# Loading the K and V cache of a decode step in two halves from two queues

## The chip, the cores and the metric

The kernel runs on one core of a Trainium2 chip. The core has five engines that run side by side: TensorE (PE in the profile, with its weight loads as PEld), VectorE (DVE), ScalarE (ACT), GpSimd (POOL) and SyncE (SP). Sixteen DMA engines move data between the device memory (HBM) and the on-chip memory. A DMA is issued by an instruction of SP, ACT or POOL and goes into that engine's DMA queue; the profile calls SP's queue q1 and ACT's q10. The metric is the device time of one execution in microseconds.

## The reference

One token goes through a layer of a transformer. With h the input row of 512 numbers and a cache of 65536 earlier positions:

```
xn = layernorm(x)                                   x: 1 x 512
q  = xn @ wq                                        32 query heads of 128, in 8 groups of 4
p  = softmax(q @ k_cache.T * 128**-0.5)             per group of 4: k_cache 65536 x 128
o  = p @ v_cache                                    v_cache 65536 x 128
h  = x + o @ wo
out = h + ((hn @ w_gate) * (hn @ w_up)) @ w_down    hn = layernorm(h), w_gate and w_up 512 x 1792
```

All of it is float32. The two caches hold 8 x 65536 x 128 numbers each, 268 MB each; they are read once and nothing of them is used twice.

## The kernel before

**Tiling.** The host puts the caches into one array of 64 chunks. For each of the 8 groups (`HKV`, called heads below) there are four K chunks and four V chunks (`NT`), each of 128 partitions times 16384 numbers: 64 KB in each partition, 8.39 MB in all. They are called K0 to K3 and V0 to V3 below. On the chip there are two buffers of that size, `kv[0]` and `kv[1]`. The even chunks go to `kv[0]`, the odd ones to `kv[1]`.

**TensorE.** Each chunk is used by 32 windows, written by `windows` (line 364): a window is 512 columns of the chunk, shows as two matmul records (64 per chunk), and window 0 comes first. A K chunk gives scores, collected in a bank of PSUM (`ps`). After the four K chunks come the softmax steps, and the weights that result (`st`, line 261) multiply the V chunks. `windows` can wait for a semaphore ahead of its first window; a chunk of K is written as windows 0 to 16, 16 to 24, 24 to 28 and 28 to 32, a chunk of V as 0 to 8, 8 to 12, 12 to 16, 16 to 24, 24 to 28 and 28 to 32. The waits between these parts are used for the last chunk and for the feed-forward weights, which come in several loads. For the other chunks one load brings the whole chunk and raises `s_k0` or `s_v0`, and POOL has raised the other semaphores (`s_k16`, `s_v16` and so on) at the start, by as much as all these chunks will take from them (line 133).

**Handing back a buffer.** When the last window of a chunk is through (`kd`), VectorE raises `free` (lines 237, 270, 279). SyncE waits for `free` and then issues the load of the chunk after next into that buffer. So there are always at most two chunks on their way or in use.

**SyncE.** SyncE's program is lines 121 and 141 to 174: the first query weights, chunks 0 and 1, then one load per `free`. Once per head it also waits for `wf` and loads `wqo_sb`, 16 KB in each partition (2.10 MB): the next head's part of `wq` and this head's part of `wo` (line 148). By its place in the loop this load goes into the queue behind the load of V1 and ahead of the load of V2. The last chunk comes in four loads (line 160), then the gate and up weights (`gu`) and the down weights (`wd`), into the same two buffers.

**ScalarE.** Per head ScalarE copies the four score banks to `sc` (line 216), each when VectorE has raised `pa` right behind `free`. Then it computes two exponentials (line 220) when VectorE has raised `da` for the first time, and two more when it has raised it for the second time, which is when V1 is through. It issues one small DMA at the start, for `x_row` (line 109).

Of the kernel before, what the change touches and what calls it, by code (L numbers as in the profile page):

```python
# [10 lines left out]
HKV, REP, DH = 8, 4, 128  # L11
SK = 65536
CK = 16384
NT = SK // CK
# [6 lines left out]
LAST = HKV - 1  # L21
PE_ONLY, DVE_ONLY, ACT_ONLY, SP_ONLY = (bass.OrderedEngineSet([e]) for e in (
    mybir.EngineType.PE, mybir.EngineType.DVE, mybir.EngineType.Activation, mybir.EngineType.SP))
SIDE = 9
LATE = 1
DVE_ACT = bass.OrderedEngineSet([mybir.EngineType.DVE, mybir.EngineType.Activation])
K_CUTS = (0, 4, 8, 12, 16, 32)
V_CUTS = (0, 8, 12, 16, 24, 28, 32)
# [14 lines left out]
def body(nc, xr, kvd, wq0, wqo, wo7, gu, wd, out):  # L43
    pe_e, dve_e, act_e, pool_e, sp = nc.tensor, nc.vector, nc.scalar, nc.gpsimd, nc.sync
# [17 lines left out]
    kv = [tile(f"kv{i}", P, CK, align=1024) for i in range(2)]  # L62
# [23 lines left out]
    def sem(name):  # L86
        sems.append(nc.alloc_semaphore(name))
        return sems[-1]
# [6 lines left out]
    pa, da, free, wf = (sem(n) for n in ("pa", "da", "free", "wf"))  # L95
    s_k0, s_k16, s_k24, s_k28 = (sem(f"s_k{i}") for i in (0, 16, 24, 28))
    s_v0, s_v8, s_v16, s_v24, s_v28 = (sem(f"s_v{i}") for i in (0, 8, 16, 24, 28))
    s_wq, s_w = sem("s_wq"), sem("s_w")
    s_wd = [sem(f"s_wd{i}") for i in range(NC - SIDE)]
    s_xr = sem("s_xr")  # L100
    late, s_act, s_pool, s_y, s_a, s_out = (sem(n) for n in ("late", "s_act", "s_pool", "s_y", "s_a", "s_out"))
    gu_t = kv[0].rearrange("p (k x) -> p k x", k=KT)[:, :, 0:2 * F]
    wd_t = kv[1]
    end = 2 * HKV * NT

    def take(e, s, n=1):
        e.wait_ge(s, n).then_inc(s, -n)  # L107
# [4 lines left out]
        inst.then_inc(own, 1)  # L112
        take(dve_e, own)

    def even(g):
        sp.dma_start(kv[0], kvd[g]).then_inc(s_k0, 16)

    def odd(g):
        sp.dma_start(kv[1], kvd[g]).then_inc(s_v0, 16)

    sp.dma_start(wq_sb, wq0).then_inc(s_wq, 16)
    pe_e.br("pe_main")
# [7 lines left out]
        out=ident, in_=ident, compare_op=ALU.not_equal, fill=1.0, base=0,  # L130
        pattern=[[-1, P]], channel_multiplier=1))
    pool.tick(pool_e.memset(qx, 0.0))
    for p, w, n in ((s_k16, 16, 0), (s_k24, 16, 0), (s_k28, 16, 0), (s_v8, 17, 0),
                    (s_v16, 16, -1), (s_v24, 16, -1), (s_v28, 16, -1)):
        pool_e.sem_inc(p, w * (end // 2 + n))
    for t in (o_pad, f_pad, sel_pad, acc, y):
        c_pads = pool.tick(pool_e.memset(t, 0.0))
    pool_e.wait_ge(s_act, 1).then_inc(s_pool, 1)
    pool_e.br("fin")

    even(0)
    odd(1)
    for g in range(2, 6):
        take(sp, free)
        (odd if g % 2 else even)(g)
    with nc.Fori(0, LAST, engines=SP_ONLY) as h:
        take(sp, wf)
        sp.dma_start(wqo_sb, wqo[h]).then_inc(s_w, 16)
        with nc.Fori(0, 2 * NT, 2, engines=SP_ONLY) as c:
            for i, put in enumerate((even, odd)):  # L150
                take(sp, free)
                put(c + (h * (2 * NT) + 6 + i))
    take(sp, wf)
    sp.dma_start(wo_sb, wo7).then_inc(s_w, 16)
    take(sp, free)
    even(end - 2)
    take(sp, free)
    for lo, hi, p in ((0, 16, s_v0), (16, 24, s_v16), (24, 28, s_v24), (28, 32, s_v28)):
        cs = slice(lo * 512, hi * 512)
# [50 lines left out]

    o_blocks = bass.AP(tensor=ptp[1].tensor, offset=0, ap=[list(ptp[1].ap[0]), [1, REP], [132, 4], [32, 4]])
    qd = qx.rearrange("p (j x) -> p j x", j=4)
    with nc.Fori(0, HKV, engines=DVE_ACT):
        for s in range(NT):
            take(act_e, pa)
            act_e.copy(sc[s], ps[s % 2]).then_inc(ad, 1)  # L216
        for n in range(0, NT, 2):
            take(act_e, da)
            for s in range(n, n + 2):
                act_e.activation(  # L220
                    ex[s - n], sc[s], AF.Exp, bias=nbias[:, 0:1], scale=SCALE,
                    accum_out=sums[:, s:s + 1]).then_inc(atok[s - n], 1)
        take(dve_e, pd)
        dve_e.tensor_copy(qrow, ptp[0][0:1, :]).then_inc(tok, 1)  # L224
        take(dve_e, pd)
        dve_e.sem_inc(wf, 1)
        q4 = sm[0][:, 0:REP]
        dve_e.tensor_copy(
            qd[:, :, 0:252].rearrange("p j (r x) -> p j r x", x=36)[:, :, :, 0:REP],
            q4.unsqueeze(1).unsqueeze(1).to_broadcast([P, 4, 7, REP])).then_inc(own, 1)  # L230
        dve_e.tensor_copy(
            qd[:, :, 252:256], q4.unsqueeze(1).to_broadcast([P, 4, REP])).then_inc(own, 1)
        take(dve_e, own, 2)
        dve_e.tensor_copy(st, qx.rearrange("p (g c) -> p g c", c=32)).then_inc(qt, 2)
        for s in range(NT):
            take(dve_e, kd, 1 + s % 2)
            dve_e.sem_inc(free, 1)
            dve_e.sem_inc(pa, 1)
            take(dve_e, ad)
            if s < 2:  # L240
                dve_e.sem_inc(qt, 1)
            dve_e.tensor_reduce(out=mx[:, s:s + 1], in_=sc[s], axis=AX.X, op=ALU.max).then_inc(own, 1)  # L242
        take(dve_e, own, NT)
        dve_e.tensor_reduce(out=m1, in_=mx, axis=AX.X, op=ALU.max).then_inc(tok, 1)  # L244
        dve_e.memset(st[:, :, 16:32], 0.0).then_inc(own, 1)
        take(dve_e, pd)
        dve_e.tensor_reduce(
            out=mrow, in_=sm[1][0:1, 0:P].rearrange("p (g h) -> p h g", h=REP), axis=AX.X,
            op=ALU.max).then_inc(own, 1)
        take(dve_e, own, 2)  # L250
        dve_e.tensor_copy(mexp, mrow.unsqueeze(1).to_broadcast([1, 32, REP])).then_inc(tok, 1)  # L251
        take(dve_e, pd)
        dve_e.tensor_scalar(
            out=nbias, in0=sm[0][:, 0:1], scalar1=-SCALE, scalar2=None, op0=ALU.mult).then_inc(da, 1)
        for n in range(NT):
            if n == 2:
                dve_e.sem_inc(tok, 2)
                take(dve_e, pd, 2)
                dve_e.sem_inc(da, 1)
            take(dve_e, pd)  # L260
            dve_e.tensor_copy(  # L261
                st[:, :, 0:16].rearrange("p g (b h) -> p b g h", h=REP),
                ptp[n % 2].rearrange("p (b g h) -> p b g h", b=4, h=REP)).then_inc(qt, 1)
            if n == NT - 1:
                mine(dve_e.tensor_reduce(out=l1, in_=sums, axis=AX.X, op=ALU.add))
                dve_e.tensor_scalar(
                    out=l4, in0=sel_h, scalar1=l1[:, 0:1], scalar2=None, op0=ALU.mult).then_inc(tok, 1)
            take(dve_e, kd, 1 + n % 2)
            if n < NT - 1:
                dve_e.sem_inc(free, 1)  # L270
            if n == 0:
                mine(dve_e.tensor_copy(orow, ps[0]))  # L272
            elif n < NT - 1:
                mine(dve_e.tensor_tensor(out=orow, in0=ps[n % 2], in1=orow, op=ALU.add))  # L274
            else:
                for cs in (slice(0, 256), slice(256, 512)):
                    dve_e.tensor_tensor(  # L277
                        out=orow[:, cs], in0=ps[1][:, cs], in1=orow[:, cs], op=ALU.add).then_inc(tob, 1)
        dve_e.sem_inc(free, 1)
        take(dve_e, pd)  # L280
        mine(dve_e.reciprocal(linv, sm[1][:, 0:REP]))
        take(dve_e, pd)
        mine(dve_e.tensor_reduce(out=ored, in_=o_blocks, axis=AX.XY, op=ALU.add))
        dve_e.tensor_tensor(out=o_pad[:, :, 0], in0=ored, in1=linv, op=ALU.mult).then_inc(tok, 1)  # L284
        take(dve_e, pd)
        for half, p in ((0, tok), (1, s_a)):
            cs = slice(half * 256, half * 256 + 256)
            dve_e.scalar_tensor_tensor(  # L288
                out=acc[:, cs], in0=attn[:, cs], scalar=1.0, in1=acc[:, cs], op0=ALU.mult, op1=ALU.add,
                accum_out=rsum[:, half:half + 1]).then_inc(p, 1)  # L290
# [40 lines left out]
    for o, g, u in ((f_pad[:, 0:1, 0], gux[0][:, 0, 3:4, 0], uf[:, 0, 1, 3:4, 0]),  # L331
                    (f_pad[:, 1:4, 0], gux[1][:, 1, 0:3, 0], uf[:, 1, 1, 0:3, 1]),
                    (f_pad[:, 4:5, 0], gux[1][:, 0, 3:4, 0], uf[:, 1, 1, 3:4, 0])):
        i = dve_e.scalar_tensor_tensor(
            out=o, in0=g, scalar=ln_r3[:, 0:1], in1=u, op0=ALU.mult, op1=ALU.mult)
# [7 lines left out]
    dve.n += 1  # L343
    assert dve.n == LATE
    dve_e.sem_inc(dve.sem, 1)
# [7 lines left out]
    for k in range(KT):  # L353
        if k == KT - 1:
            pe_e.wait_ge(s_wq, 16)
        i = pe_e.transpose(ps[0][:, k:k + 1], xn_row[0:1, k * P:(k + 1) * P], ident[0:1, 0:1])
# [35 lines left out]
    for k in range(KT):  # L392
        i = mm(ptp[0][0:1, :], xn[:, k:k + 1], wq_sb[:, k, :], start=(k == 0), stop=(k == KT - 1))  # L393
    i.then_inc(pd, 1)
    pe_e.wait_ge(tok, 4)
    for r in range(REP):
        i = pe_e.transpose(sm[0][:, r:r + 1], qrow[0:1, r * P:(r + 1) * P], ident[0:1, 0:1])  # L397
# [13 lines left out]
    for half in range(2):  # L411
        pe_e.wait_ge(atok[half], 1)
        for b in range(4):
            i = pe_e.transpose(ptp[half][:, b * P:(b + 1) * P], ex[half][:, b * P:(b + 1) * P], ident)  # L414
# [9 lines left out]
    for half in range(2):  # L424
        step()
        for b in range(2):
            i = pe_e.transpose(ptp[half][:, b * P:(b + 1) * P],
                               gu_sb[:, (2 * half + b) * P:(2 * half + b + 1) * P], ident)
# [25 lines left out]
    for b in range(4):  # L454
        if b < 3:
            pe_e.wait_ge(*((tob, 1), (s_w, 16), (tob, 2))[b])
        i = pe_e.transpose(ptp[1][:, b * P:(b + 1) * P], orow[:, b * P:(b + 1) * P], ident)  # L457
    i.then_inc(pd, 1)
    pe_e.wait_ge(tok, 2)
    for r in range(REP):  # L460
        i = mm(attn[32 * r:32 * r + 32, :], o_pad[:, r, :], wo_sb[:, r, :],  # L461
               start=True, stop=True)
# [6 lines left out]
    for k in range(KT):  # L469
        if k % 2 == 0:  # L470
            pe_e.wait_ge(*((s_a, HKV) if k else (tok, 3)))
        i = pe_e.transpose(ptp[1][:, k * P:(k + 1) * P], acc[:, k * P:(k + 1) * P], ident)
# [69 lines left out]
```

## Time and profile before

| | |
|---|---|
| time, median of 3 runs | 1308.68 us (1308.65 to 1309.05) |
| span of the profiled execution, first to last instruction | 1307.4 us |
| between that span and the median of the runs | 1.3 us |
| bytes read from HBM | 564.66 MB |
| packets on SP's queue q1 / on ACT's queue q10 | 12848 / 2 |
| busy PE, DVE, ACT, POOL | 686.2, 111.6, 54.9, 2.7 us |
| PE waiting for a K or V load (line 364) | 520.1 us, 58 times |

The page gives the span of the profiled execution and no separate time for it; the runs' times lie 1.3 us above that span. A DMA issue has a row of its own (SPq or ACTq); its time is that of the issuing instruction, not of the transfer. When a chunk has landed is seen from the row of line 364 that had waited for it. "Packets" are the pieces that the DMA engines recorded.

### The profile page before, as it was taken

How to read it: one execution, taken by the hardware profiler on the slowest of the kernel's cores; microseconds unless marked ns; L12 is line 12 of the kernel's file. 1: busy time of each engine (PE TensorE's matmuls, PEld its weight loads, DVE VectorE, ACT ScalarE, POOL GpSimd, SP SyncE). 2: the span in 40 equal slices, each digit the busy share in tenths (PEclk: the TensorE clock that was granted, in tenths of full speed). 3: DMA queues.
4: the chain of work that ended last, by engine and by line, in shares of the span. 5: the costliest groups of instructions: out<-in, count | busy, mean ns of one | idle time of the engine just before them, and what ended most of it. 6: DMA issues, size and time to landing. Idle time of an engine off the chain costs nothing. (4 is left out here: it accounts for less than half of the span.)

```text
span 1307.4 us, 10833 instructions
## 1 busy us (share of the span) xinstructions
PE 686.2 (52%) x4610; PEld 191.5 (15%) x4610; DVE 111.6 (9%) x286; ACT 54.9 (4%) x106; POOL 2.7 (0%) x12
## 2 busy tenths in 40 slices
PE   4456364453654545553554636535566445545557
PEld 1011111110111111111110211101111111111112
DVE  1000010100101001000010101001010010100101
ACT  0000000000000000000000000000000000000000
POOL 0000000000000000000000000000000000000000
PEclk8676796776976768767787767868677677877679
DMA  9999999999999999999999999999999999999999
GB/s 417 421 445 429 437 447 419 449 417 449 417 449 417 449 417 449 421 445 427 439 439 427 449 417 449 417 449 417 449 417 449 417 434 440 441 437 429 447 408 382
DMA packets 12850, 564.72 MB, mean 432 GB/s; under 512 B 1409, under 2 KB 1457, under 8 KB 2610
## 3 DMA queue, kind: packets, MB, share of 16 engines
q1 hardware_dynamic: 12848, 564.71, 99.8%
q10 hardware_dynamic: 2, 0.00, 0.0%
HBM read 564.66 MB, written 0.05 MB: 432 GB/s over the span
## 5 line engine op out<-in xcount | busy, mean ns | idle before, releaser
L364 PE MATMUL ps<-kv,st 128*32 128x512 f32 x4184 | 591.0, 728 | 534.6 <-DMA kv<-in_kv 520.1
L364 PEld LDWEIGHTS ps<-kv,st 128*32 128x32 f32 x4184 | 146.7, 131 | 962.3 <-DMA kv<-in_kv 568.1
L242 DVE TENSOR_REDUCE mx<-sc 128x1 f32<-128x512 f32 x32 | 21.9, 686 | 535.9 <-DVEq L107 535.9
L414 PE MATMUL ptp<-ident,ex 128*128 128x128 f32 x128 | 27.3, 372 | 19.8 <-ACT ex L220 19.5
L216 ACT COPY sc<-ps 128x512 f32<-128x512 f32 x32 | 18.8, 586 | 444.6 <-ACTq L107 444.5
L274 DVE TENSOR_TENSOR orow<-ps,orow 128x512 f32<-128x512 f32 x16 | 11.1, 691 | 298.3 <-DVEq L107 298.3
L220 ACT ACTIVATE ex<-sc,nbias 128x512 f32<-128x512 f32 x32 | 22.8, 714 | 304.4 <-ACTq L107 304.4
L393 PE MATMUL ptp<-wqo_sb,xn 128*1 128x512 f32 x64 | 30.4, 620 | 6.4 <-DVE acc L288 5.0
L216 ACT ACT_TABLE_LOAD x8 | 10.3, 1283 | 441.5 <-ACTq L107 441.5
L261 DVE COPY st<-ptp 128x512 f32<-128x512 f32 x32 | 22.1, 692 | 44.5 <-DVEq L107 44.5
L414 PEld LDWEIGHTS ptp<-ident,ex 128*128 128x128 f32 x128 | 20.2, 188 | 22.9 <-ACT ex L220 22.8
L407 PE MATMUL sm<-ident,m 128*1 128x128 f32 x16 | 4.5, 283 | 27.2 <-DVE m L244 17.6
L277 DVE TENSOR_TENSOR orow<-ps,orow 128x256 f32<-128x256 f32 x16 | 6.0, 419 | 129.3 <-DVEq L107 129.3
L272 DVE COPY orow<-ps 128x512 f32<-128x512 f32 x8 | 5.5, 692 | 102.0 <-DVEq L107 102.0
L461 PE MATMUL attn<-wqo_sb,o_pad 128*32 128x512 f32 x64 | 8.5, 605 | 5.9 <-DVE o_pad L284 5.9
L409 PE MATMUL sm<-ones,mexp 1*128 1x1 f32 x32 | 6.9, 281 | 6.7 <-DVE mexp L251 6.7
L393 PEld LDWEIGHTS ptp<-wqo_sb,xn 128*1 128x1 f32 x64 | 4.9, 85 | 30.9 <-issue 18.1
L224 DVE COPY qrow<-ptp 1x512 f32<-1x512 f32 x8 | 5.4, 679 | 29.7 <-DVEq L107 29.7
L457 PE MATMUL ptp<-ident,orow 128*128 128x128 f32 x32 | 6.1, 300 | 3.0 <-DVE orow L277 3.0
L407 PEld LDWEIGHTS sm<-ident,m 128*1 128x1 f32 x16 | 1.3, 79 | 41.8 <-DVE m L244 24.9
L288 DVE SCALAR_TENSOR_TENSOR acc<-attn,acc 128x256 f32<-128x256 f32 x16 | 6.2, 421 | 10.8 <-DVEq L107 10.8
L397 PE MATMUL sm<-ident,qrow 1*128 1x1 f32 x32 | 3.2, 201 | 7.1 <-DVE qrow L224 7.1
(84 smaller groups left out, 78.4 us busy)
## 6 DMA issues: line engine op xcount, KB each, us to landing
wqo_sb<-in_wqo SPq DMA_DIRECT2D x7, 2048.0 KB, 32.9
kv<-in_kv SPq DMA_DIRECT2D x1, 4096.0 KB, 22.2
kv<-in_gu SPq DMA_DIRECT2D x1, 3584.0 KB, 17.6
kv<-in_kv SPq DMA_DIRECT2D x1, 2048.0 KB, 26.7
kv<-in_kv SPq DMA_DIRECT2D x2, 1024.0 KB, 29.7
kv<-in_gu SPq DMA_DIRECT2D x1, 1792.0 KB, 21.4
kv<-in_wd SPq DMA_DIRECT2D x1, 1536.0 KB, 19.0
kv<-in_wd SPq DMA_DIRECT2D x5, 256.0 KB, 20.5
```

The costliest lines, as they stand in the source:

```text
L216: act_e.copy(sc[s], ps[s % 2]).then_inc(ad, 1)
L220: act_e.activation(ex[s - n], sc[s], AF.Exp, bias=nbias[:, 0:1], scale=SCALE, accum_out=sums[:, s:s + 1]).then_inc(atok[s - n], 1)
L242: dve_e.tensor_reduce(out=mx[:, s:s + 1], in_=sc[s], axis=AX.X, op=ALU.max).then_inc(own, 1)
L261: dve_e.tensor_copy(st[:, :, 0:16].rearrange("p g (b h) -> p b g h", h=REP), ptp[n % 2].rearrange("p (b g h) -> p b g h", b=4, h=REP)).the ...
L274: mine(dve_e.tensor_tensor(out=orow, in0=ps[n % 2], in1=orow, op=ALU.add))
L288: dve_e.scalar_tensor_tensor(out=acc[:, cs], in0=attn[:, cs], scalar=1.0, in1=acc[:, cs], op0=ALU.mult, op1=ALU.add, accum_out=rsum[:, hal ...
L364: i = mm(ps[buf][32 * j:32 * j + 32, :], st[:, 8 * j + r, :], kv[buf][:, w * 512:(w + 1) * 512], start=(r == 0), stop=(r in (2, 3, 7)), sk ...
L393: i = mm(ptp[0][0:1, :], xn[:, k:k + 1], wq_sb[:, k, :], start=(k == 0), stop=(k == KT - 1))
L409: mm(sm[0][:, 0:1], mexp.rearrange("p g h -> p (g h)"), ones[0:1, 0:1], start=True, stop=True).then_inc(pd, 1)
L414: i = pe_e.transpose(ptp[half][:, b * P:(b + 1) * P], ex[half][:, b * P:(b + 1) * P], ident)
L457: i = pe_e.transpose(ptp[1][:, b * P:(b + 1) * P], orow[:, b * P:(b + 1) * P], ident)
L461: i = mm(attn[32 * r:32 * r + 32, :], o_pad[:, r, :], wo_sb[:, r, :], start=True, stop=True)
```

## The change

The loads of chunks 2 to 61 are each cut into two loads of 32 KB per partition, columns 0 to 8191 and 8192 to 16383. SyncE still waits for `free`; it then raises a new semaphore `af` and issues the first half, which raises `s_k0` or `s_v0`. ScalarE waits for `af` and issues the second half, which raises `s_k16` or `s_v16`, so that windows 16 and on now wait for a load of their own. Chunks 0, 1 and 62 are cut in the same way, but both loads come from SyncE. Chunk 63 and the feed-forward weights stay as they were.

ScalarE's loop over the heads becomes a function: behind each copy of scores it issues the second half of the chunk that is loaded in that place, and behind each pair of exponentials those of two chunks more. The last head is written out behind the loop because its V chunks free buffers for loads that SyncE issues alone. VectorE's loop is a loop of its own now, with the same instructions. POOL no longer raises `s_k16` and `s_v16` at the start.

```diff
-    def even(g):
-        sp.dma_start(kv[0], kvd[g]).then_inc(s_k0, 16)
-
-    def odd(g):
-        sp.dma_start(kv[1], kvd[g]).then_inc(s_v0, 16)
+    def both(g):
+        for lo, p in ((0, (s_k0, s_v0)[g % 2]), (HALF, (s_k16, s_v16)[g % 2])):
+            sp.dma_start(kv[g % 2][:, lo:lo + HALF], kvd[g][:, lo:lo + HALF]).then_inc(p, 16)
...
-    for p, w, n in ((s_k16, 16, 0), (s_k24, 16, 0), (s_k28, 16, 0), (s_v8, 17, 0),
-                    (s_v16, 16, -1), (s_v24, 16, -1), (s_v28, 16, -1)):
+    for p, w, n in ((s_k24, 16, 0), (s_k28, 16, 0), (s_v8, 17, 0),
+                    (s_v24, 16, -1), (s_v28, 16, -1)):
...
-    even(0)
-    odd(1)
+    both(0)
+    both(1)
+
+    def first_half(g, i):
+        take(sp, free)
+        sp.sem_inc(af, 1)
+        sp.dma_start(kv[i][:, 0:HALF], kvd[g][:, 0:HALF]).then_inc((s_k0, s_v0)[i], 16)
+
+    def second_half(g, i):
+        take(act_e, af)
+        act_e.dma_start(kv[i][:, HALF:CK], kvd[g][:, HALF:CK]).then_inc((s_k16, s_v16)[i], 16)
+
     for g in range(2, 6):
-        take(sp, free)
-        (odd if g % 2 else even)(g)
+        first_half(g, g % 2)
...
-            for i, put in enumerate((even, odd)):
-                take(sp, free)
-                put(c + (h * (2 * NT) + 6 + i))
+            for i in range(2):
+                first_half(c + (h * (2 * NT) + 6 + i), i)
...
-    even(end - 2)
+    both(end - 2)
...
-    with nc.Fori(0, HKV, engines=DVE_ACT):
+    def act_head(h, last):
         for s in range(NT):
             take(act_e, pa)
             act_e.copy(sc[s], ps[s % 2]).then_inc(ad, 1)
+            second_half(h * (2 * NT) + 2 + s, s % 2)
         for n in range(0, NT, 2):
             take(act_e, da)
...
+            for s in range(n, n + 2):
+                if not last:
+                    second_half(h * (2 * NT) + 6 + s, s % 2)
+
+    with nc.Fori(0, LAST, engines=ACT_ONLY) as h:
+        act_head(h, False)
+    act_head(LAST, True)
+    with nc.Fori(0, HKV, engines=DVE_ONLY):
```

More of the change, by code (lines that the diff above doesn't have):

```diff
@@ L25 @@
 LATE = 1
+HALF = CK // 2
 DVE_ACT = bass.OrderedEngineSet([mybir.EngineType.DVE, mybir.EngineType.Activation])
@@ L100, in body @@
     s_xr = sem("s_xr")
+    af = sem("af")
     late, s_act, s_pool, s_y, s_a, s_out = (sem(n) for n in ("late", "s_act", "s_pool", "s_y", "s_a", "s_out"))
```

## The prediction

> **What bounds the kernel now.** I read the page's slices first, then the time windows, the table of waits, and last the timeline of single chunks. Head of the page, busy times, DMA share of the 40 slices, and traffic:
>
> ```profile
> span 1307.4 us, 10833 instructions
> PE 686.2 (52%) x4610; PEld 191.5 (15%) x4610; DVE 111.6 (9%) x286; ACT 54.9 (4%) x106; POOL 2.7 (0%) x12
> DMA  9999999999999999999999999999999999999999
> DMA packets 12850, 564.72 MB, mean 432 GB/s; under 512 B 1409, under 2 KB 1457, under 8 KB 2610
> q10 hardware_dynamic: 2, 0.00, 0.0%
> HBM read 564.66 MB, written 0.05 MB: 432 GB/s over the span
> ```
>
> Windows (length, busy times, granted clock, DMA share, GB/s) and waits:
>
> ```profile
> 44.20:1246.80 1202.60, 631.55 (x4251) 175.08 (x4251) 95.39 (x228) 49.94 (x98) 0.00 (x0) 0.74 1.00 434
> 223.17:242.45 19.28, 9.25 (x65) 2.27 (x65) 0.69 (x1) 0.59 (x1) 0.00 (x0) 0.77 1.00 435
> 1259.40:1299.60 40.20, 31.41 (x220) 9.29 (x220) 6.75 (x31) 0.00 (x0) 0.00 (x0) 0.88 1.00 425
> PE ps L364 <- DMA kv<-in_kv: 520.1, 58, 12.1
> SPq L107 <- SPq L107: 1225.3, 66, 32.5
> ```
>
> The DMA engines are busy in every slice, at 434 GB/s over 1202 us and 435 within one chunk. PE waits for a load 58 times, 520 us in all, so the engines that compute are not the limit; the bytes are. Timeline, chunks K1 to V3 of the second head:
>
> ```profile
> 223.17 9.25 PE L364 MATMUL ps<-kv,st 128*32 128x512 f32 x64 [10.63 <-DMA kv<-in_kv]
> 232.96 0.33 SPq L116 DMA_DIRECT2D kv<-in_kv  x1
> 242.45 9.85 PE L364 MATMUL ps<-kv,st 128*32 128x512 f32 x64 [10.03 <-DMA kv<-in_kv]
> 252.72 0.59 ACT L216 COPY sc<-ps 128x512 f32<-128x512 f32 x1 [19.29 <-ACTq L107]
> 252.81 0.33 SPq L119 DMA_DIRECT2D kv<-in_kv  x1
> 253.90 0.33 SPq L148 DMA_DIRECT2D wqo_sb<-in_wqo  x1
> 256.62 0.72 ACT L220 ACTIVATE ex<-sc,nbias 128x512 f32<-128x512 f32 x1 [3.31 <-ACTq L107]
> 281.17 9.26 PE L364 MATMUL ps<-kv,st 128*32 128x512 f32 x64 [10.66 <-DMA kv<-in_kv]
> 290.94 0.33 SPq L119 DMA_DIRECT2D kv<-in_kv  x1
> 292.49 0.72 ACT L220 ACTIVATE ex<-sc,nbias 128x512 f32<-128x512 f32 x1 [34.35 <-ACTq L107]
> 305.30 9.14 PE L364 MATMUL ps<-kv,st 128*32 128x512 f32 x64 [10.59 <-DMA kv<-in_kv]
> 314.98 0.33 SPq L116 DMA_DIRECT2D kv<-in_kv  x1
> ```
>
> A chunk lands 19.28 us after the one before (223.17 to 242.45). Between V1 (281.17) and V2 (305.30) it is 24.13, because the 2.10 MB of `wqo_sb` go in between: 4.85 us more, the same rate although its rows are 16 KB and not 64 KB. From a landing to the next issue it is 9.77 us (V1) and 9.68 us (V2). At that issue the other chunk still has some 9.6 us of transfer to go. **This 9.6 us is the whole reserve of the kernel**: DMA never idles because that much is queued whenever a load is added. Time is bytes over 435 GB/s, plus every gap in which the queues run empty.
>
> **The change part by part.** The bytes stay: 60 chunks as 2 x 4.19 MB, each half 9.65 us of transfer when alone (half of 19.28).
>
> *Instructions.* SP issues as many loads as before and 60 increments more; it waits 1225 us. POOL drops two increments. ACT gets 60 waits and 60 issues; its one issue so far, in the rows of the start, took 0.53 us:
>
> ```profile
> 0.74 0.53 ACTq L109 DMA_DIRECT2D x_row<-in_xr  x1
> 2.13 0.67 DVE L182 TENSOR_REDUCE ln_s<-x_row 1x1 f32<-1x512 f32 x1 [0.88 <-DMA x_row<-in_xr]
> 16.46 0.69 DVE L234 COPY st<-qx 128x1024 f32<-128x1024 f32 x1
> 24.92 9.39 PE L364 MATMUL ps<-kv,st 128*32 128x512 f32 x64 [9.20 <-DMA kv<-in_kv]
> 34.62 0.33 SPq L116 DMA_DIRECT2D kv<-in_kv  x1
> 34.72 1.28 ACT L216 ACT_TABLE_LOAD   x1 [28.45 <-ACTq L107]
> 36.02 0.59 ACT L216 COPY sc<-ps 128x512 f32<-128x512 f32 x1
> 44.26 9.96 PE L364 MATMUL ps<-kv,st 128*32 128x512 f32 x64 [9.95 <-DMA kv<-in_kv]
> wqo_sb<-in_wq SPq DMA_DIRECT2D x1, 1024.0 KB, 4.8
> ```
>
> 60 x 0.53 = 32 us on an engine that is busy for 55. Queued behind the new wait are the next copy and the exponentials. Behind K3 the issue can end at about 253.9 (copy from 252.72, then 0.53) and the exponential starts at 256.62: 2.7 us of cover. Behind V1 the `af` comes at 290.94 and the exponential starts at 292.49: 0.53 of 1.55 us. Were the cover gone, PE would wait 0.5 us ahead of V2, inside its 10.6 us wait for that load. The second half enters the queue later than the first by the copy, 0.59 us, behind K0 by 1.28 + 0.59 = 1.87; the 9.6 us of queued work hide that. **Cost: nothing.**
>
> *Start.* Chunk 0's first half lands 9.65 us earlier, at 15.3; PE can start at 17.2 (`st` ready), so K0 is through some 4.7 us sooner, and chunk 2's second half, on the empty queue of ACT, runs beside chunk 1. That makes chunk 1 up to 9.65 us later than its 44.26 and chunk 2 as much further along: nothing gained, nothing lost, but **the second halves are ahead from then on.**
>
> *Two queues in the DMA engines.* In the trace q10 carries 2 packets, so how an engine divides itself between two queues with work is not shown; I take it from both sides. What the trace does show is the unit: 12850 packets less 1409 below 512 B are 11441, exactly one per contiguous row of all loads (8576 of K and V, 896 of `wqo_sb`, 1969 others). A row of 64 KB goes as one packet. A packet of a half is 32 KB, at 435/16 = 27.2 GB/s 1.2 us; one of `wqo_sb` is 16 KB, 0.6 us.
>
> Take V1 landed at time 0. SP's queue holds `wqo_sb`, then V2's first half; ACT's holds V2's second half. V3's halves come when V1 is through: 9.7 us, plus issue and landing latency. For that the first load has 4.8 us less 2.4 for its 1.05 MB, 2.4 us; the lower end is the 2 KB `x_row`, 2.13 - 0.74 = 1.4. I take 2.4, the load of the same kind: 12.1 us.
>
> - *By bytes:* `wqo_sb` and half of V2's second half until 9.7; at 19.3 that half is done and the first half is half done; shared with V3's second half it lands at 29.0. Then 4.19 + 2.10 MB, 14.5 us, are queued, and the next chunk needs 12.1. No gap: **+0.**
> - *By turns of whole packets:* while 8 packets of `wqo_sb` go on an engine, all 8 of V2's second half go too, 14.5 us. V2's first half then shares with V3's second half, which has been queued since 12.1, and both end at 33.8. Now only V3's first half is queued, 9.65 us; K0 of the next head needs 12.1. **Gap 12.1 - 9.65 = 2.45 us**, or 1.25 where one packet of V3's second half is still out. The first head has the full gap (second halves already ahead), later ones start level after each gap: 2.45 + 6 x 1.25 = 10.0 us.
> - *By turns of whole loads* V2's first half can be passed by V3's second half in the same way, on every other head as the turns alternate: 4 x 2.45 = 9.8 us.
>
> I take turns, **+10.0 us**: the packet is what the engine records, and nothing in the trace shows one being cut. The low end is 1.45 + 6 x 0.25 = 3 us (latency 1.4); for the high end the slowest V2, 1102.36 to 1112.87, 10.51 us:
>
> ```profile
> 1102.36 9.97 PE L364 MATMUL ps<-kv,st 128*32 128x512 f32 x64 [11.46 <-DMA kv<-in_kv]
> 1112.87 0.33 SPq L116 DMA_DIRECT2D kv<-in_kv  x1
> ```
>
> 7 x (10.51 + 2.4 - 9.65) = 23 us. A gap isn't made up later, as nothing runs above 435 GB/s.
>
> [...]
>
> *End.* Chunk 62 in two loads and all behind it stay on SP's queue in the old order. Cost nothing.
>
> **Sum**, against the profiled span of 1307.4 us and the 1.3 us by which the median of the runs is above it: 1308.7 + 10.0 = **1318.7 us.**
>
> **The rivals.**
>
> *Not slower: shares by bytes, or in order of issue.* Works as in the first case: the spare is 14.5 - 12.1 = 2.4 us at the worst place, so no gap: **1308.7.** [...] It decides if the shares differ by less than 2.4 us at V3. [...]
>
> *A queue first.* If q1 goes first, chunk 62 passes 61's second half; SP then waits for that half's windows (about 4.9 us) and 2.4 us of latency: +7.3, **1316.0.** If q10 goes first, every second chunk leaves only one first half queued: up to 30 gaps of 2.45, +73, **1382.** Nothing speaks for either.
>
> *Changing queues costs the engine time.* The low end is 0, by the 4.85 us of `wqo_sb`. The high end is the stretch with rows of 2 to 64 KB, 425 against 435 GB/s: 2.3% of 1220 us, +28, **1337.**
>
> *Faster.* It would take a gap that exists now, or more than 435 GB/s. The stretch of 1202 us at share 1.00 leaves neither; only some 2.5 us at the start could move: **1306.**
>
> **How the numbers follow.** Turns with gaps 0.52, bytes or order of issue 0.33, a queue first 0.05, cost of changing 0.07, faster 0.03. The two large cases lie on both sides of the bound, 0.2% or 2.6 us, about what a measurement of this kernel tells from no change. Slower: 0.50 + 0.05 + 0.05 = 0.60; same: 0.33 and the small ends of two cases, 0.36; faster 0.04. The likeliest case alone spans 1312 to 1326; taking in no change, the range is 1308.0 to 1326.
>
> **What would show it.** In the windows, a DMA share below 1.00 in a stretch of a few us, once per head near the landing of V2 and before the next head's K0 is queued, 7 times, and 434 GB/s elsewhere. Rows of line 364 for V2 start some 34 us after V1's, not 24; window 16 does not wait there, since the second half is early. V3 follows within 10 us. If V2 comes 29 us after V1, the shares are by bytes, and the time is unchanged. If the rate between gaps is below 434, changing queues costs. The prediction is wrong if no slice loses DMA share, or if gaps come at other chunks.

## The result, and the profile after

| | before | after |
|---|---|---|
| median | 1308.66 us (1308.57 to 1309.05, 4 runs) | 1332.62 us (1331.21 to 1333.32, 4 runs) |
| ratio | 1 | 1.0181, 95% interval 1.0168 to 1.0194 |
| span of the profiled execution | 1307.4 us | 1331.9 us |

The change costs 24.0 us. The forecast was slower by 10.0 us, to 1318.7, with a range that ended at 1326.0: the direction was right, the size was not.

The page of the changed kernel: span, busy times, DMA share in slices, packets and queues (packets, MB, share of 16 engines' span), and the `wqo_sb` loads (KB, us from issue to landing; 32.9 before).

```profile
span 1331.9 us, 11132 instructions
PE 693.3 (52%) x4610; PEld 195.3 (15%) x4610; DVE 111.5 (8%) x286; ACT 53.6 (4%) x105; POOL 2.7 (0%) x12
DMA  9999999999999999999999999999999999999999
...
DMA packets 21924, 564.74 MB, mean 424 GB/s; under 512 B 2417, under 2 KB 2465, under 8 KB 3618
...
q1 hardware_dynamic: 13280, 313.05, 54.6%
q10 hardware_dynamic: 8642, 251.66, 44.1%
...
wqo_sb<-in_wqo SPq DMA_DIRECT2D x7, 2048.0 KB, 42.6
```

The bytes are the same, and no digit of the DMA row shows the loss: a slice of 33 us at "9" hides a stop of 3 us. The shares of the queues show it. Before, q1 had all of the traffic:

```profile
q1 hardware_dynamic: 12848, 564.71, 99.8%
```

54.6 + 44.1 = 98.7% of 1331.9 us are 1314.6 us of packet time per engine, against 99.8% of 1307.4 (1304.8 us) before: some 10 us more of recorded packet time, and the time without a packet grew from 2.6 to 17.3 us. PE's wait for loads at line 381 (line 364 before) grew by only 13.6 us, of which more below:

```profile
PE ps L381 <- DMA kv<-in_kv: 533.7, 59, 21.5
```

Its longest wait went from 12.1 to 21.5 us. The timeline of the changed kernel, V0 to V3 of the first head, then K0 of the second, shows where that stands:

```profile
104.24 8.39 PE L381 MATMUL ps<-kv,st 128*32 128x512 f32 x64 [2.57 <-DMA kv<-in_kv]
123.64 8.93 PE L381 MATMUL ps<-kv,st 128*32 128x512 f32 x64 [11.01 <-DMA kv<-in_kv]
157.54 9.04 PE L381 MATMUL ps<-kv,st 128*32 128x512 f32 x64 [20.69 <-DMA kv<-in_kv]
167.15 0.37 ACTq L151 DMA_DIRECT2D kv<-in_kv  x1
167.21 0.33 SPq L147 DMA_DIRECT2D kv<-in_kv  x1
168.68 7.07 PE L381 MATMUL ps<-kv,st 128*32 128x512 f32 x64 [2.09 <-PEq L109]
189.13 8.61 PE L381 MATMUL ps<-kv,st 128*32 128x512 f32 x64 [4.51 <-DMA kv<-in_kv]
```

V2 comes 33.9 us after V1 (24.13 in the second head before), all 32 windows at once: its second half was there long before. V3 is on the chip by the time PE is ready for it, 11 us later, which is why PE's total wait hardly moves. The price is paid between them. Windows of the changed kernel (length, busy times, granted clock, DMA share, GB/s of packets that start in it): the time around the next issue, then 5 us of each head at the same place.

```profile
159.80:162.20 2.40, 2.40 (x20) 0.59 (x16) 0.00 (x0) 0.00 (x0) 0.00 (x0) 0.63 1.01 437
164.60:165.80 1.20, 1.20 (x16) 0.36 (x12) 0.00 (x0) 0.00 (x0) 0.00 (x0) 1.00 0.20 82
165.80:167.00 1.20, 0.79 (x8) 0.00 (x0) 0.10 (x1) 0.00 (x0) 0.00 (x0) 1.00 0.00 0
167.00:168.20 1.20, 0.00 (x0) 0.00 (x0) 0.94 (x2) 0.00 (x0) 0.00 (x0) 1.00 0.62 164
168.20:169.40 1.20, 0.72 (x8) 0.34 (x12) 0.63 (x3) 0.00 (x0) 0.00 (x0) 1.00 0.91 273
169.40:171.80 2.40, 2.40 (x28) 0.91 (x24) 0.00 (x0) 0.00 (x0) 0.00 (x0) 1.00 1.01 437
```

```profile
165.00:170.00 5.00, 2.91 (x30) 0.77 (x25) 1.68 (x4) 0.00 (x0) 0.00 (x0) 1.00 0.40 118
328.00:333.00 5.00, 2.91 (x28) 0.70 (x24) 1.68 (x4) 0.00 (x0) 0.00 (x0) 0.92 0.40 111
491.00:496.00 5.00, 2.91 (x28) 0.97 (x28) 1.67 (x4) 0.00 (x0) 0.00 (x0) 1.00 0.64 216
653.00:658.00 5.00, 2.91 (x21) 0.62 (x17) 1.68 (x4) 0.00 (x0) 0.00 (x0) 0.85 0.54 170
816.00:821.00 5.00, 2.91 (x28) 0.78 (x24) 1.67 (x4) 0.00 (x0) 0.00 (x0) 0.93 0.39 111
979.50:984.50 5.00, 2.91 (x32) 1.13 (x32) 1.67 (x4) 0.00 (x0) 0.00 (x0) 1.00 0.79 288
1141.00:1146.00 5.00, 2.91 (x24) 0.62 (x20) 1.67 (x4) 0.00 (x0) 0.00 (x0) 0.86 0.48 157
```

The engines work at 437 GB/s until V3's first half is through, then stand still until the two issues of 167.2 take effect. It happens in all 7 heads that have a `wqo_sb` load. The seven shares miss 3.36 x 5 = 16.8 us in all; the first packets after a stop are slow too (168.20 to 169.40: share 0.91 at 273 GB/s), which the share counts as busy. The stops are not of one length, because the next issue waits until PE is through V2: in the fifth head PE takes 9.94 us for V2's windows and the window misses 3.05 us, in the sixth 8.37 us and 1.05.

### The profile page after: what moved, and what is told of

Read it like the earlier page. It is cut to its first block, busy times and chain, and to the rows that moved or that the text cites. A ratio compares the mean times of both kernels' runs of the same rounds, so it can differ in the third digit from the quotient of the medians.

```text
span 1331.9 us, 11132 instructions
## 1 busy us (share of the span) xinstructions
PE 693.3 (52%) x4610; PEld 195.3 (15%) x4610; DVE 111.5 (8%) x286; ACT 53.6 (4%) x105; POOL 2.7 (0%) x12
## 3 DMA queue, kind: packets, MB, share of 16 engines
q1 hardware_dynamic: 13280, 313.05, 54.6%
q10 hardware_dynamic: 8642, 251.66, 44.1%
## 5 line engine op out<-in xcount | busy, mean ns | idle before, releaser
L431 PE MATMUL ptp<-ident,ex 128*128 128x128 f32 x128 | 28.0, 382 | 19.8 <-ACT ex L229 19.6
## 6 DMA issues: line engine op xcount, KB each, us to landing
kv<-in_wd SPq DMA_DIRECT2D x1, 1536.0 KB, 19.4
```

## The experiments

Ratios are against runs of the kernel before on the same chip (1308.81 us beside the first four, 1308.77 beside the last three).

**Both halves from one queue.**

```diff
         take(sp, free)
-        sp.sem_inc(af, 1)
         sp.dma_start(kv[i][:, 0:HALF], kvd[g][:, 0:HALF]).then_inc((s_k0, s_v0)[i], 16)
+        sp.dma_start(kv[i][:, HALF:CK], kvd[g][:, HALF:CK]).then_inc((s_k16, s_v16)[i], 16)
     def second_half(g, i):
-        take(act_e, af)
-        act_e.dma_start(...)
+        pass
```

> All loads of K and V stay cut in halves, but SyncE issues both halves, first then second, so only one queue has work. Theory G (the loss is idle gaps of the DMA engines once per head, behind wqo_sb, plus a small price per packet): no gap is possible in one queue, only the packets remain, 504 more per engine at 8 ns (two of 1.213 us against one of 2.418), 4 us, and half a microsecond for the completions: 1312 to 1314. Theory Q (two queues with work at once cost the engines time): nothing is left, 1308.7 to 1309.5. Theory S (cutting a load costs by itself, whatever the queue): 1323 or more.

Measured 1311.47 us, ratio 1.0020 (1.0011 to 1.0029): 2.7 us. Its queues, with the same number of packets as the changed kernel:

```profile
DMA packets 21924, 564.74 MB, mean 431 GB/s; under 512 B 2417, under 2 KB 2465, under 8 KB 3618
...
q1 hardware_dynamic: 21920, 564.72, 100.0%
```

Cutting the loads is not what costs 24 us. What is left fits a price of more packets, somewhat under what theory G gave.

**The price of a packet by itself.** One queue, one load per chunk, rows of 16 KB.

```diff
-        sp.dma_start(kv[0], kvd[g]).then_inc(s_k0, 16)
+        sp.dma_start(four(kv[0]), kvd[g]).then_inc(s_k0, 16)
...
+    def four(a):
+        return a.rearrange("p (a x) -> p a x", a=4)
...
+    arrays["kv"] = np.concatenate([arrays["kv"], arrays["kv"][..., 0:64]], axis=3)
```

> The kernel before the change: one queue, one load per chunk. Only the array in HBM is laid out with 256 bytes between quarters of a row, so that a load has 4 rows of 16 KB per partition in place of one of 64 KB. It measures the price of a packet by itself: 3 more packets per row, 63 x 8 x 3 = 1512 per engine. By the durations in the trace, 4 x 0.611 - 2.418 = 26 ns per row: 13 us, 1320 to 1323. If packets cost nothing and only bytes count: 1308.7.

Measured 1315.83 us, ratio 1.0053 (1.0040 to 1.0066), below the expected range: 7.0 us for 1512 more packets per engine, 4.6 ns each. With one queue and halves it was 2.7 us for 504, 5.3 ns with the extra completions (a packet of 4 B on each engine at the end of a load). The two prices are close, and both lie at a little over half of what the packets' recorded durations gave. The page shows why these can't simply be added up: the packets' time comes to more than the span.

```profile
DMA packets 37170, 564.72 MB, mean 429 GB/s; under 512 B 1409, under 2 KB 1457, under 8 KB 2610
...
q1 hardware_dynamic: 37168, 564.71, 100.2%
```

**The weights divided over both queues.**

```diff
         take(sp, wf)
-        sp.dma_start(wqo_sb, wqo[h]).then_inc(s_w, 16)
+        sp.sem_inc(af, 1)
+        sp.dma_start(wqo_sb[:, 0], wqo[h][:, 0]).then_inc(s_w, 16)
...
             second_half(h * (2 * NT) + 2 + s, s % 2)
+        take(act_e, af)
+        act_e.dma_start(wqo_sb[:, 1], wqo[h][:, 1]).then_inc(s_w, 16)
```

(The last head divides `wo7` likewise, and PE waits for 32.)

> The changed kernel, with the 2.10 MB of wqo_sb divided: its wq half is issued by SyncE, its wo half by ScalarE, 8 packets of 8 KB per engine in each queue, so the queues stay level. Theory G: V2 lands 24.2 us after V1 as before the change, no DMA idle at V2, time 1312.5 to 1315. Theory Q: the idle goes but the packets stay slow, 1318 to 1323. A third, theory L (the gaps come from ScalarE issuing its halves late): the gaps stay, 1330 or more.

Measured 1312.83 us, ratio 1.0030 (1.0019 to 1.0041). Of the changed kernel's 24 us this takes away 19.8 (1332.62 - 1312.83), 2.8 us for each of 7 heads. V1, V2 and V3 of its first head, and 5 us behind V2:

```profile
123.34 9.06 PE L388 MATMUL ps<-kv,st 128*32 128x512 f32 x64 [10.86 <-DMA kv<-in_kv]
147.61 8.87 PE L388 MATMUL ps<-kv,st 128*32 128x512 f32 x64 [10.93 <-DMA kv<-in_kv]
166.97 9.43 PE L388 MATMUL ps<-kv,st 128*32 128x512 f32 x64 [10.49 <-DMA kv<-in_kv]
```

```profile
163.00:168.00 5.00, 1.03 (x8) 0.38 (x12) 0.00 (x0) 0.00 (x0) 0.00 (x0) 0.50 1.03 446
```

V2 is back at 24.3 us after V1, and DMA does not stop. ScalarE issues its halves as late as in the changed kernel, so theory L falls. Two queues with work at all times, kept level, cost little: 1.4 us more than one queue with the same halves.

**The weights in ScalarE's queue.**

```diff
         take(sp, wf)
-        sp.dma_start(wqo_sb, wqo[h]).then_inc(s_w, 16)
+        sp.sem_inc(af, 1)
...
             second_half(h * (2 * NT) + 2 + s, s % 2)
+        take(act_e, af)
+        act_e.dma_start(wqo_sb, wqo[h]).then_inc(s_w, 16)
```

> The changed kernel, with all of wqo_sb issued by ScalarE in place of SyncE, so the second halves fall behind and not the first. Theory G in its full form (a gap is what the next load needs, consumption plus latency, less the 9.65 us that is queued): the windows 0 to 15 of V2 are done when its second half lands some 34 us after V1, so the next load needs 4.9 + 2.4 = 7.3 us and there is no gap: 1313 to 1316. The simpler rival (any load of this size in one of the two queues empties the other and costs a gap): the 7 gaps stay, 1330 or more.

Measured 1319.13 us, ratio 1.0069 (1.0050 to 1.0088), single runs from 1311.9 to 1321.9: between the two, in neither range. Second head, V1, then V2 in two parts, the next issue, and 6 us around it:

```profile
285.54 8.39 PE L386 MATMUL ps<-kv,st 128*32 128x512 f32 x64 [9.86 <-DMA kv<-in_kv]
300.04 6.23 PE L386 MATMUL ps<-kv,st 128*32 128x512 f32 x32 [1.82 <-DMA kv<-in_kv]
319.28 5.15 PE L386 MATMUL ps<-kv,st 128*32 128x512 f32 x32 [13.01 <-DMA kv<-in_kv]
325.00 0.35 ACTq L151 DMA_DIRECT2D kv<-in_kv  x1
```

```profile
323.00:329.00 6.00, 3.90 (x40) 1.18 (x36) 1.68 (x4) 0.00 (x0) 0.00 (x0) 1.00 0.93 366
```

The mirror image is there: V2's second half lands 33.7 us after V1, with 16 of its windows done, and the next load is issued 5.7 us after that landing and not 9.6. The long stop is gone, and at the same place in the next five heads the share is 0.97 to 1.02 (398 to 426 GB/s); but the margin, 9.65 - 7.3 = 2.3 us by the expectation, did not bring the time to the expected 1313 to 1316. The packet records show one reason: the 16 engines do not work in step. The completions of V2's second half lie between 314.9 and 318.9, those of V3's between 325.7 and 328.6; in the kernel before those of a chunk lie within 0.5 us (280.28 to 280.76 for V1). V2's windows 16 and on started at 319.28, behind the slowest engine; the fastest had ended its part 4.0 us before. The spread is shown; that it alone made the 6 us is argued.

**The first half handed back early.** `lf` is a new semaphore that TensorE raises.

```diff
-        take(sp, free)
-        sp.sem_inc(af, 1)
+        take(sp, lf)
         sp.dma_start(kv[i][:, 0:HALF], kvd[g][:, 0:HALF]).then_inc((s_k0, s_v0)[i], 16)
+        take(sp, free)
+        sp.sem_inc(af, 1)
...
-    windows(0, 0, 16, s_k0)
+    windows(0, 0, 16, s_k0).then_inc(lf, 1)
...
-    windows(1, 12, 16)
+    windows(1, 12, 16).then_inc(lf, 1)
```

> The changed kernel, wqo_sb all in SyncE's queue again, but the first half of a buffer is handed back as soon as the windows 0 to 15 are through: TensorE signals SyncE itself, some 5 us before free; the second half still waits for free. Theory G (a gap is what the next load needs after the landing of V2, less what is still queued): behind V2 the next first half now needs 4.9 us and some 2 us of latency, under 9.65, so no gap: 1312 to 1315, in spite of V2 landing 34 us after V1. Rival (unequal queues cost time by themselves, gap or not): 1325 or more.

Measured 1312.62 us, ratio 1.0030 (1.0020 to 1.0041), as expected. V1 and V2 of the first head, and the next two issues:

```profile
121.70 9.41 PE L382 MATMUL ps<-kv,st 128*32 128x512 f32 x64 [10.52 <-DMA kv<-in_kv]
155.60 9.52 PE L382 MATMUL ps<-kv,st 128*32 128x512 f32 x64 [19.60 <-DMA kv<-in_kv]
162.07 0.33 SPq L146 DMA_DIRECT2D kv<-in_kv  x1
165.69 0.34 ACTq L152 DMA_DIRECT2D kv<-in_kv  x1
```

```profile
162.00:167.00 5.00, 3.12 (x32) 0.67 (x24) 1.31 (x3) 0.00 (x0) 0.00 (x0) 1.00 0.98 406
```

This is the strongest of the tests: the queues are as unequal as in the changed kernel, V2 still lands 33.9 us after V1, and the time is gone all the same. Unequal queues cost little by themselves: 1312.62 us against the 1312.83 of the level ones. The next load came 6.5 us after the landing and not 9.6, before the 9.65 us of queued work were used up.

**Both together.**

The two edits above in one kernel.

> The divided wqo_sb of the second run together with the early return of the first half. With divided weights alone 1312.8 were left, and chunk 3 came 20.8 us after chunk 2 where 19.4 is usual. Theory: that 1.4 us is a first gap at the start, where K1 is late and the queue behind K2 is short; with the early return it goes, and only the price of the packets is left, as with one queue: 1311.3 to 1312.0. If two queues at once cost engine time: 1312.8 or more.

Measured 1312.16 us (1312.06 to 1312.30), ratio 1.0025 (1.0015 to 1.0036). Chunks 2 and 3 of the kernel with only the weights divided, then of this one:

```profile
63.80 9.81 PE L388 MATMUL ps<-kv,st 128*32 128x512 f32 x64 [3.64 <-DMA kv<-in_kv]
84.61 9.65 PE L388 MATMUL ps<-kv,st 128*32 128x512 f32 x64 [11.00 <-DMA kv<-in_kv]
```

```profile
63.60 9.59 PE L389 MATMUL ps<-kv,st 128*32 128x512 f32 x64 [3.80 <-DMA kv<-in_kv]
82.98 7.58 PE L389 MATMUL ps<-kv,st 128*32 128x512 f32 x56 [9.79 <-DMA kv<-in_kv]
```

The distance shrinks from 20.8 to 19.4 us, so the small loss at the start is real, and the early return takes it away. The median fell by only 0.7 us, half of that, and 0.2 above the expected range. The runs with divided weights alone go from 1312.1 to 1313.9, and the profiled one, in which the 20.8 stands, was the slowest; how many of the others had that loss is not known. What remains above one queue, 0.7 us, is not settled. 72 more packets per engine from the divided weights, at the 4.6 to 5.3 ns above, would be 0.3 to 0.4 us of it, an estimate.

**ScalarE's half second.**

```diff
         take(sp, free)
-        sp.sem_inc(af, 1)
         sp.dma_start(kv[i][:, 0:HALF], kvd[g][:, 0:HALF]).then_inc((s_k0, s_v0)[i], 16)
+        sp.sem_inc(af, 1)
```

> The changed kernel with two lines exchanged: SyncE raises af behind its own load, so ScalarE's half enters its queue some 0.4 us later than SyncE's and not 0.06 us earlier as at the restart behind a gap (167.15 and 167.21). Theory O (which half leads by a packet is settled by who is first after a gap, and it takes away or leaves one packet of V3's second half as cover): each gap from the second head on is a packet, 1.2 us, shorter, 6 x 1.2 = 7 us: 1324 to 1327. Rival (the order at the restart doesn't matter): 1331 to 1334.

Measured 1329.10 us, ratio 1.0161 (1.0144 to 1.0177): 3.5 us less than the changed kernel, half of what theory O gave and more than nothing, in the range of neither theory. The same places in the first four heads:

```profile
164.00:169.00 5.00, 2.90 (x28) 0.81 (x24) 1.68 (x4) 0.00 (x0) 0.00 (x0) 1.00 0.60 210
325.00:330.00 5.00, 2.49 (x12) 0.60 (x16) 1.68 (x4) 0.00 (x0) 0.00 (x0) 0.71 0.97 360
489.00:494.00 5.00, 2.90 (x32) 0.97 (x28) 1.68 (x4) 0.00 (x0) 0.00 (x0) 1.00 0.63 229
650.50:655.50 5.00, 2.80 (x28) 0.94 (x32) 1.09 (x4) 0.00 (x0) 0.00 (x0) 1.00 0.97 413
```

A head with a long stop alternates with one that has hardly any; the other three shares are 0.80, 0.95 and 0.59. So the order at the restart does matter, but not by one packet as theory O had it. Behind the first stop the first packets of the two halves are 4.2 us apart (166.35 and 170.53), and in the second, fourth and sixth head V3's second half ends 4.8 us behind V2's first half (313.86 and 318.70 in the second): four packets of cover, and next to no stop. In the heads between it ends only 1.2 to 2.8 us behind, and there the stop is back. That a head without a stop lets the queues drift to this place is argued. The seven shares miss 7.5 us against 16.8, yet the medians differ by 3.5 only (the two profiled runs by 5.4), so some of this kernel's loss lies outside these windows and is not explained.

## Why the prediction was wrong, point by point

**The bound** was read right. Bytes over 435 GB/s (436 between 125 and 163 us of the changed kernel) plus gaps, with the price of packets below, accounts for the time after as for the time before. The 9.6 us of reserve is the measure that decides: the early return of the first half brought the next load inside it, and the gaps were gone.

**Turns of whole packets** were right. V2 was forecast at 33.8 us after V1 by packets and 29.0 by bytes; it came at 33.9. The packet records of the first head show the turns: from 138 to 152 us each queue starts 15 or 16 packets in every 2.4 us, one per engine by turns, and while `wqo_sb` goes a row of 16 KB counts for as much as a row of 32 KB: from 121.36 to 136.59 us, where its 128 rows go, the other queue starts 129. Turns of whole loads, the prediction's third case, are not what these records show. Two level queues cost 1.4 us against one where the next load came in time; the changed kernel, in which the queues ran out, took 19.8 us more than that. The rival by bytes, at 0.33, was wrong in its premise.

**The step that failed is the size of the gap term,** 2.45 + 6 x 1.25 = 10.0 us where the division of the weights took away 19.8. The sum gave the first head the full gap, since the second halves were to be "ahead from then on", and the other six 1.25, since these were to "start level after each gap" with "one packet of V3's second half" still out as cover. The records show it the other way round. In the first head the lead that the second halves had with K2 (ends at 51.18 and 63.35) was lost by K3 (84.53, with the first half at 83.32), and V3's second half ended a packet behind V2's first half. In the later heads, behind a stop, ScalarE's issue is first by 0.06 us (167.15 and 167.21), its packets go first, and the second halves stay ahead from there. Packet records of the changed kernel, the end of the last packet of each half:

| | V2 first half | V3 second half | V3 first half | first packet of K0 |
|---|---|---|---|---|
| head 1 | 155.95 | 157.16 | 166.84 | 168.15 |
| head 2 | 319.21 | 319.32 | 329.01 | 331.18 |
| head 3 | 482.32 | 481.11 | 492.01 | 492.94 |
| head 4 | 644.33 | 643.95 | 654.01 | 655.85 |

In heads 2 to 7 (the last three not in the table) V3's second half ends with V2's first half or before it: no packet is left as cover, and 9.65 us is all there is. With the cover put where it was, the prediction's own sum is 1.25 + 6 x 2.45 = 16.0 us; the full gap in every head is 17.2, and the shares above miss 16.8. That these two agree so well is in part luck: from V2's last packet to K0's first one it is 12.2, 12.0, 10.6 and 11.5 us in the table, where the sum had 12.1 for every head. The first head missed 3.0 us in spite of its packet of cover; its engines were apart there, with the completions of V2's first half spread over 3.1 us, against 0.5 in the second head. That the spread used up the cover is argued.

The sum also lacked a term, the restart. Behind each of the seven stops the first packet of an engine takes 1.8 to 1.9 us (medians) where packets of a half otherwise take 1.21, 4.6 us over the seven stops by the means. The 16.8 and the 4.6 come to a little more than the 19.8; no run tries the restart alone.

**The price of more packets was put at nothing** ("Instructions", "the bytes stay"). It is some 2.7 us by the run with one queue. The row that I took as proof, 4.85 us for `wqo_sb`, covers 8 packets per engine, 8 x 5 ns = 0.04 us: it could not have shown it. The rival for changing queues stayed at its low end: 0.7 us above one queue in the run with both edits.

**The start, "nothing gained, nothing lost",** lost up to 1.4 us, by the distance of chunks 2 and 3. I checked that the bytes were the same and not whether the reserve lasted; K1 was through so late that chunk 3's second half was issued at 60.86, when K2's last packet was to end at 63.35.

**ScalarE's issues** cost next to nothing, as forecast: with both edits ScalarE issues even more loads, and the time is within 0.7 us of one queue.

The runs give 2.7 us from the kernel before to one queue with halves, 1.4 from there to two level queues and 19.8 from there to the changed kernel. These are steps along one chain of runs, so that they come to 23.9 of 24.0 us tests nothing; what each step means rests on the runs and windows above.

None of the seven kernels beats the kernel before. It has no gap to close (q1's packets take 99.8% of the 16 engines' span) and the largest packets (64 KB).

## What to carry to other kernels

In a kernel bound by transfers, work out for every landing how much is still queued and how long it takes until the next load's first packet. In the changed kernel that was 10.6 to 12.2 us, in the four heads of the table, against 9.65 queued, and DMA stopped in all 7 heads; with the next issue 6.5 us after the landing in place of 9.6 the time was 1312.62 us. A margin of 2.3 us, by the estimate, did not hold with the weights in ScalarE's queue (1319.13 us). Two queues were served in turns by packets here, so give both the same number of packets between two landings, extra loads included: with `wqo_sb` in one queue V2 came 33.9 us after V1, with `wqo_sb` divided 24.3. And take a favourable detail, such as who is one packet ahead, into a sum only if something in the program holds it there.

## What was not expected of the hardware

- A packet had a price of its own per engine: 4.6 ns for those of 16 KB, 5.3 ns for those of 32 KB with the completions counted in.
- The 16 engines drifted apart in some runs: with divided weights the completions of one half lay 3.2 us apart (304.38 to 307.60), against 0.5 us in the kernel before. Two queues alone don't do it: with both edits it was 0.7 us for most loads. In the changed kernel and with divided weights the spread begins at K3, at the place of the loss at the start, which both edits take away; that the one makes the other is not shown. With the weights in ScalarE's queue a margin of 2.3 us stood beside spreads of 4.0 and 2.9 us, and time was lost; what a reserve below the spread costs was not tried alone.
- Behind the seven stops the first packets were slow: 1.8 to 1.9 us in place of 1.21, and in the first head 273 GB/s in the second stretch of 1.2 us in which packets went again.
